# All tap products ahead of the fifth half product, sums of y ahead of the output, and a product's copy split over two buffers

## The chip, the cores and the metric

The kernel runs on one core of a Trainium2 chip. The metric is the device time of one execution in microseconds (us). The kernel before takes 988.49 us, the median of three runs (987.34 to 989.33). The profiled execution, from which all other times here come, has a span of 988.2 us and a mean granted TensorE clock of 0.999.

## The reference

The input x has shape (8, 4224, 192). A causal depthwise convolution with 7 taps, softmax-normalised and one set for each of 8 heads of 24 channels, gives y. Then comes a layer normalisation without bias, a matrix product with w_ch1 (192 x 768), a ReLU, a product with w_ch2 (768 x 192), and y is added again.

```python
# convolution: 7 taps of one head for its 24 channels, softmax over the taps
out = np.einsum('hk,bskhg->bshg', softmax(weight), windows(x_pad))
# mixer
xn = (y - mean(y)) / np.sqrt(var(y) + 1e-06) * g_ln
return y + np.maximum(xn @ w_ch1, 0.0) @ w_ch2
```

All is float32. The kernel folds g_ln and the mean into w_ch1 once, and multiplies by the reciprocal standard deviation only after the second product, since a positive factor passes through the ReLU.

## The kernel before

The rows are cut into 18 groups (numbered 0 to 17); from group 4 on a group is 16 rows on each of 128 partitions. Groups 5 to 16 are called MIXED (line 81), and the change acts on them. The schedule is written by hand: each engine carries out its instructions in the order of the source, and waits only for data and for buffers.

The work on one group g is spread over three rounds of the main loop (line 891). In round g-2 ScalarE makes the first tap product of each head (`first_tap`, line 376, into y) and the second one (`second_tap`, line 393, into the buffer tb), 16 instructions in all, and two DMAs with accumulation then add tb to y (line 403; "y<-tb" in the profile). In round g-1 VectorE adds the other five taps to y (`conv`, line 408), transposes y (`transpose`, line 419) and takes the moments of its rows. In round g TensorE carries out both matrix products.

`up_mixed` (line 591) is the first matrix product of a MIXED group. It is a seven-product scheme on 2 x 2 blocks. The blocks of y are a11 to a22, the precomputed sums of y are s1, s2, s3 (`sums_of_y`, line 575), and the sums of w_ch1 are in w1sums. The steps, numbered 1 to 9 here, are: 1 a11 x b11; 2 a12 x b21; 3 s2; 4 s3; 5 s1; 6 a22; 7 s2 again; then 8 and 9, two plain products for the columns that the scheme leaves out. The steps use two sets of four PSUM banks in turn: 1, 3, 5, 7 and 9 the set `chain`, and 2, 4, 6 and 8 the set `other`. ScalarE copies each result out of its set (`evict`, line 610), and a step can't begin before the copy two steps ahead of it has ended. Steps 2, 5 and 6 are copied to side buffers, from which a DMA with accumulation adds them to a block of the hidden tile `room` (`close`, line 614):

- step 2 to `first`, which lies in the buffer tagged tb, the buffer that the second tap products of another group use too;
- step 5 to `second`, in the buffer tagged cs, which also holds the output columns in `down_fast`;
- step 6 to `first` again.

Each of these two buffers holds three slots of 1024 elements a partition, of which `first` and `second` take two.

`down_fast` (line 714) is the second matrix product, again seven products. Each is a half product of 72 matrix instructions in the profile, numbered 1 to 7 here, and each result but the fourth is copied out by ScalarE in three copies (line 739). Between the half products ScalarE makes tap products of group g+2, as many as `taps_behind` says (line 758). After the fourth, VectorE transposes y of group g+1, and makes the nine `half_sum`s (line 698) that half products 5 to 7 read. After the fifth, `close_by_dma` adds `part` to the block c21 of the output ("cs<-part" in the profile). `finish_fast` (line 796) transposes the output columns from cs to the tile ot, in two halves; the first half needs cs<-part, and the second half (line 801) reads a part that half product 6 left in `room`, which step 3 of the next `up_mixed` writes over. ScalarE scales the rows of ot (line 828) inside the next `up_mixed`, and a DMA with accumulation adds them to the result.

All DMAs with accumulation are issued by GpSimd, in the order of the source.

Of the kernel before, what the change touches and what calls it, by code (L numbers as in the profile page):

```python
# [16 lines left out]
def kernel(  # L17
# [32 lines left out]
    H, K = weight.shape  # L50
# [12 lines left out]
    NQ = P // C  # L63
# [18 lines left out]
    PAIR = NF // 2 - 1  # L82
# [28 lines left out]
    bpool = ctx.enter_context(tc.tile_pool(name="tb", bufs=1))  # L111
    cpool = ctx.enter_context(tc.tile_pool(name="cs", bufs=1))
# [64 lines left out]
    room = hpool.tile([P, NF * J * P], F32, tag="ht", name="room")  # L177
# [213 lines left out]
    tb = {}  # L391
# [16 lines left out]
    def conv(g, k0=1, k1=K, heads=(0, H)):  # L408
        n = groups[g][2]
        t = xg[g]  # L410
        for k in range(k0, k1):
            for h in range(*heads):
                cs = slice(h * GRP, h * GRP + GRP)
                nc.vector.scalar_tensor_tensor(  # L414
                    out=y[g][:, 0:n, cs], in0=t[:, k : k + n, cs], scalar=taps[:, h, k : k + 1],
                    in1=y[g][:, 0:n, cs], op0=ALU.mult, op1=ALU.add,
                )
# [173 lines left out]
    def up_mixed(g, last_sum):  # L591


        W = HJ * C
        assert groups[g][2] == fast[g] == 2 * HJ and PAIR * W == 512
        hidden_tile(g)
        a = ht[g][0]
        a11, a12, a21, a22 = quarters_of_y(g)
        b11, b12, b21, b22 = quarters_of_w1()
        s1, s2, s3 = ysums[g]  # L600
        (c11, c12), (c21, c22) = [
            [a[:, h, e, 0:PAIR].rearrange("p f q j t -> p f q (j t)") for e in range(2)]
            for h in range(2)
        ]

        def parts(pool, tag):
            room = pool.tile([P, J * D], F32, tag=tag, name=f"parts_{tag}{g}")
            return room[:, 0 : PAIR * NQ * W].rearrange("p (f q w) -> p f q w", q=NQ, w=W)

        def evict(banks, dst, relu=False):  # L610
            src = banks.rearrange("p q (f w) -> p f q w", w=W)
            nc.scalar.activation(dst, src, AF.Relu) if relu else nc.scalar.copy(dst, src)  # L612

        def close(c, part):
            whole = "p f q w -> p (f q w)"
            add_by_dma(c.rearrange(whole), part.rearrange(whole))

        def plain(f, banks):
            rows_of_tiles(banks, yt[g][:, 0 : 2 * HJ], w1[:, :, f * P : f * P + P])
            evict_up(g, f, slice(0, 2 * HJ), banks)  # L620


        chain, other = take_set(), take_set()
        turn[0] += 4
        done = groups[g - 1][2]
        first, second = parts(bpool, "tb"), parts(cpool, "cs")
        rows_of_tiles(chain, a11, b11, True, False)
        evict(chain, c11)
        rows_of_tiles(other, a12, b21)
        evict(other, first)  # L630
        close(c11, first)
        rows_of_tiles(chain, s2, w1sums[:, 1], False, False)
        evict(chain, c21)
        scale(g - 1, 0, 1)
        conv(g + 1, 2, 3)
        next(last_sum)
        rows_of_tiles(other, s3, w1sums[:, 2], True, False)
        evict(other, c22)
        scale(g - 1, 1, 2)
        rows_of_tiles(chain, s1, w1sums[:, 0], False, False)  # L640
        evict(chain, second)
        close(c22, second)
        scale(g - 1, 2, 3)
        rows_of_tiles(other, a22, w1sums[:, 3], False)
        evict(other, first)
        close(c21, first)
        scale(g - 1, 3, 4)
        rows_of_tiles(chain, s2, b22, False)
        evict(chain, c12, True)
        nc.scalar.activation(c11, c11, AF.Relu)  # L650
        scale(g - 1, 4, 7)
        conv(g + 1, 3, 6)
        plain(PAIR, other)
        nc.scalar.activation(c22, c22, AF.Relu)
        scale(g - 1, 7, 10)
        add_to_out(g - 1, 0, 8)
        lower_sum(g, (PAIR,))
        lower_sum(g, range(PAIR))
        conv(g + 1, 6, K)
        plain(PAIR + FC, chain)  # L660
        scale(g - 1, 10, done)
        add_to_out(g - 1, 8, done)
# [51 lines left out]
    def down_fast(g):  # L714
        n = fast[g]
        t = width(g)
        w = n * T
        a = ht[g][0]
        flat = cpool.tile([P, NC, NFAST * C], F32, tag="cs", name=f"cs{g}")[:, :, 0 : n * C]
        order = "p c (h j t) -> p c h j t" if t == C else "p c (j h t) -> p c h j t"  # L720
        cs = flat.rearrange(order, h=2, t=t)
        part = cpool.tile([P, CH, NFAST * T], F32, tag="part", name=f"part{g}")[:, :, 0:w]
        part = part.rearrange("p c (j t) -> p c j t", t=t)

        parts = [part, a[:, 1, 0].rearrange("p f q j t -> p (f q) j t")[:, 0:CH]]
        banks = [take_bank() for c in range(CH) for i in range(2)]

        def product(bank, left, right, to, first):
            for c in range(CH):
                dst = banks[2 * c + bank]  # L730
                for f in range(FC):
                    for q in range(NQ):
                        nc.tensor.matmul(  # L733
                            dst[C * q : C * q + C, 0:w], right[:, f, C * c : C * c + C],
                            left[:, f, q], start=(first and f == 0), stop=(f == FC - 1),
                            skip_group_check=True,
                        )
                if to is not None:
                    nc.scalar.copy(  # L739
                        to[:, c], dst[:, 0:w].rearrange("p (j t) -> p j t", t=t)  # L740
                    )

        b = quarters_of_w2()
        c11, c21 = cs[:, 0:CH, 0], cs[:, 0:CH, 1]
        c12, c22 = cs[:, CH:NC, 0], cs[:, CH:NC, 1]
        todo = [(tap, h) for tap in (first_tap, second_tap) for h in range(H)] if g + 2 < NG else []

        def close_by_dma(c, part):
            add_by_dma(*(v.rearrange("p c j t -> p c (j t)") for v in (c, part)))

        def some_taps(times):
            for tap, h in todo[:times]:
                tap(g + 2, heads=(h, h + 1))
            del todo[:times]

        taps_behind = [3, 3, 3, 3, 2, 2]
        if g in MIXED:
            taps_behind = [1, 4, 4, 5, 2, 0]
        elif g + 1 in MIXED:
            taps_behind = [4, 4, 4, 4, 0, 0]  # L760
        product(0, a[:, 0, 0], b[0], c11, True)
        some_taps(taps_behind[0])
        product(1, a[:, 1, 0], w2sums[:, 2], c22, True)
        some_taps(taps_behind[1])
        product(1, a[:, 1, 1], w2sums[:, 3], parts[0], False)
        some_taps(taps_behind[2])
        product(1, a[:, 0, 1], b[2], None, True)
        some_taps(taps_behind[3])
        if g in MIXED:
            transpose(g + 1)  # L770
            moments(g + 1, 0, EARLY)
        elif g + 1 in MIXED:
            moments(g + 1)
            if g + 1 == MIXED[0]:
                sums_of_quarters(w1sums, *quarters_of_w1())
        half_sum(g, (1, 1), (1, 1), (1, 0), ALU.add)
        half_sum(g, (0, 0), (1, 1), (0, 0), ALU.add)
        half_sum(g, (0, 1), (0, 1), (1, 1), ALU.subtract)
        for c in range(CH):
            nc.vector.tensor_tensor(  # L780
                c11[:, c], c11[:, c], banks[2 * c + 1][:, 0:w].rearrange("p (j t) -> p j t", t=t),
                op=ALU.add,
            )
        product(0, a[:, 1, 1], w2sums[:, 1], c21, False)
        if g + 1 == NG:
            finish_fast(g, 0, flat, cs, parts)
        if g in MIXED:
            close_by_dma(c21, parts[0])
        some_taps(taps_behind[4])
        product(0, a[:, 0, 0], w2sums[:, 0], parts[1], False)  # L790
        some_taps(taps_behind[5])
        product(0, a[:, 0, 1], b[3], c12, False)
        some_taps(len(todo))
        return flat, cs, parts
# [96 lines left out]
    for g in range(NG):  # L891
        if g + 2 < NG and g not in (3, 4):
            load_x(g + 2)
        mixed, last = g in MIXED, g + 1 == NG
# [41 lines left out]
        parts = down_fast(g)  # L936
# [6 lines left out]
        if mixed:  # L943
            moments(g + 1, EARLY)
        later = sums_of_y(g + 1) if g + 1 in MIXED else iter(())
        if not last:
            finish_fast(g, 0, *parts)
            next(later, None)
        finish_fast(g, 1, *parts)
        if not last and not mixed and g + 1 not in MIXED:  # L950
            moments(g + 1)
        if not last and g % 2 == 0:
# [35 lines left out]
```

## Time and profile before

| engine | busy us | share of the span | instructions |
|---|---|---|---|
| TensorE, matmul | 969.5 | 98% | 16050 |
| VectorE | 854.3 | 86% | 1477 |
| ScalarE | 623.3 | 63% | 1034 |
| GpSimd | 178.0 | 18% | 317 |

| transfer, issued by GpSimd | issues | KB each | median us from issue to landing |
|---|---|---|---|
| y<-tb | 28 | 768 | 9.1 |
| room<-parts_tb | 24 | 1024 | 9.3 |
| room<-parts_cs | 12 | 1024 | 7.5 |
| cs<-part | 12 | 384 | 4.5 |

In the profile PE is TensorE, PEld its weight loads, ACT ScalarE, DVE VectorE, POOL GpSimd and SP the engine that only issues DMAs. L612 is line 612 of the kernel. A name such as parts_tb<-ps says which tile is written and which is read; ps is PSUM. A row of the waits gives the engine and line that waited, the engine and line (or transfer) that ended the wait, and then the total in us, the number of waits and the longest. A row of the timeline gives the start in us, the us it took, the engine, line and operation, and in brackets the idle time ahead of it with what ended it.

### The profile page before, as it was taken

Reading aid. Unit: us, or ns where it says so; the run is one execution under the profiler, and the core shown is the slowest. Engines: PE = TensorE matmul, PEld = TensorE weight load, DVE = VectorE, ACT = ScalarE, POOL = GpSimd, SP = SyncE. Lnnn points to the kernel's source line nnn. Section 1 sums busy time; section 2 is a strip of 40 time slices with the busy share of each in tenths; the row PEclk is TensorE's granted clock in tenths of the full one; section 3 lists DMA queues with packets and bytes.
Section 4 is the critical chain, followed back from the end, with each engine's and each line's share of the span. In section 5 each row is a group of like instructions: output and inputs, shape, how many; then the busy total and the mean of one; then the engine's idle time right before and its main releaser. Section 6 shows DMA issues by size and latency. Waiting matters only on the chain.

```text
span 988.2 us, 35674 instructions
## 1 busy us (share of the span) xinstructions
PE 969.5 (98%) x16050; PEld 659.8 (67%) x16050; DVE 854.3 (86%) x1477; ACT 623.3 (63%) x1034; POOL 178.0 (18%) x317
## 2 busy tenths in 40 slices
PE   7999999999999999999999999999999999999997
PEld 6886445556758585766758576676857566685787
DVE  6999886899899898989999898989989898998507
ACT  5625646364867758585875858586685848675451
POOL 2002500115111041112211041111301141110200
PEclk9999999999999999999999999999999999999999
DMA  8233752664797869779677977969696786675141
GB/s 201 95 121 130 116 164 36 209 157 130 139 250 145 239 130 191 194 153 253 143 219 145 208 178 143 260 131 241 143 236 148 147 237 135 160 147 93 18 67 67
DMA packets 26279, 156.07 MB, mean 158 GB/s; under 512 B 3215, under 2 KB 8591, under 8 KB 17294
## 3 DMA queue, kind: packets, MB, share of 16 engines
q0 software_dynamic: 19456, 96.25, 50.3%
q1 hardware_dynamic: 6366, 57.54, 15.2%
q8 instruction: 126, 2.06, 0.8%
q14 instruction: 27, 0.22, 0.1%
q10 hardware_dynamic: 304, 0.00, 0.0%
HBM read 38.95 MB, written 50.33 MB: 90 GB/s over the span
## 4 chain that ended last, share of the span: by engine, by line
issue 44%; PE 32%; DMA 11%; POOL 8%; DVE 4%; ACT 2%; POOLq 0%; SPq 0%; ACTq 0%; DVEq 0%
PE ps L532 16%; PE ps L733 11%; DMA y<-tb 7%; PE ps L680 5%; DVE y L414 3%; DMA xg<-in_x_dram 2%; POOL room L589 2%; POOL out_dram L835 2%; POOL cs L589 1%; ACT parts_tb L612 1%; POOL y L403 1%; DMA room<-parts_tb 1%; POOL d L458 1%; DMA ga<-in_moe_g_ln_dram 0%; DVE room L698 0%
## 5 line engine op out<-in xcount | busy, mean ns | idle before, releaser
L414 DVE SCALAR_TENSOR_TENSOR y<-xg,taps,y 128x384 f32<-128x384 f32 (+4 forms) x734 | 368.1, 579 | 12.1 <-issue 8.9
L532 PE MATMUL ps<-yt,w 32*128 32x512 f32 (+5 forms) x4320 | 334.2, 461 | 2.9 <-ACT parts_tb L612 1.9
L532 PEld LDWEIGHTS ps<-yt,w 32*128 32x128 f32 x4320 | 213.7, 185 | 116.5 <-issue 95.4
L733 PE MATMUL ps<-room,w2sums 128*32 128x256 f32 (+2 forms) x4320 | 233.7, 374 | 0.4 <-issue 0.3
L733 PEld LDWEIGHTS ps<-room,w2sums 128*32 128x32 f32 x4320 | 140.9, 110 | 87.7 <-DVE room L698 2.3
L698 DVE TENSOR_TENSOR room<-room 128x1024 f32<-128x1024 f32 (+2 forms) x144 | 160.4, 1186 | 42.0 <-ACT part L739 23.3
L733 PE MATMUL ps<-room,w 128*32 128x256 f32 (+2 forms) x3240 | 179.3, 374 | 0.0
L733 PEld LDWEIGHTS ps<-room,w 128*32 128x32 f32 x3240 | 104.6, 110 | 72.8 <-ACT ot L828 9.1
L739 ACT COPY cs<-ps 128x256 f32<-128x256 f32 (+2 forms) x180 | 63.3, 366 | 111.8 <-PE ps L733 111.1
L522 ACT ACTIVATE room<-ps 128x2048 f32<-128x2048 f32 (+4 forms) x54 | 79.8, 1477 | 55.2 <-PE ps L532 55.1
L532 PE MATMUL ps<-ysums,w1sums 32*128 32x256 f32 x1728 | 98.4, 377 | 4.0 <-ACT parts_tb L612 4.0
L828 ACT ACTIVATE ot<-ot,r 128x192 f32<-128x192 f32 x248 | 96.2, 448 | 0.0
L532 PEld LDWEIGHTS ps<-ysums,w1sums 32*128 32x128 f32 x1728 | 87.5, 185 | 12.8 <-ACT parts_tb L612 8.3
L612 ACT COPY room<-ps 128x2048 f32<-128x2048 f32 x36 | 67.3, 1868 | 39.6 <-PE ps L532 37.1
L707 DVE SCALAR_TENSOR_TENSOR room<-room 128x1024 f32<-128x1024 f32 x36 | 43.0, 1223 | 45.0 <-ACT room L522 24.5
L387 ACT ACTIVATE y<-xg,taps 128x384 f32<-128x384 f32 (+4 forms) x137 | 71.7, 590 | 11.2 <-DMA out_dram<-y 8.5
L835 POOL DMA_DIRECT2D out_dram<-ot x40 | 34.0, 1077 | 238.2 <-ACT ot L828 187.6
L441 DVE BATCH_NORM_STATS2 st<-y 128x6 f32<-128x192 f32 x264 | 70.8, 342 | 0.0
L612 ACT COPY parts_tb<-ps 128x2048 f32<-128x2048 f32 x24 | 44.8, 1866 | 27.3 <-DMA y<-tb 18.5
L803 DVE STREAM_TRANSPOSE ot<-cs 128x512 f32<-128x512 f32 (+2 forms) x90 | 55.8, 670 | 6.2 <-DMA cs<-part 3.7
L425 DVE STREAM_TRANSPOSE yt<-y 128x3072 f32<-128x3072 f32 (+4 forms) x19 | 56.2, 2957 | 5.1 <-PE ps L532 3.0
L400 ACT ACTIVATE tb<-xg,taps 128x384 f32<-128x384 f32 x112 | 59.5, 605 | 0.0
(104 smaller groups left out, 702.4 us busy)
## 6 DMA issues: line engine op xcount, KB each, us to landing
xg<-in_x_dram SPq DMA_DIRECT2D x12, 2112.0 KB, 14.8
room<-parts_tb POOLq DMA_DIRECT2D x24, 1024.0 KB, 9.3
y<-tb POOLq DMA_DIRECT2D x28, 768.0 KB, 9.1
out_dram<-ot POOLq DMA_DIRECT2D x27, 768.0 KB, 7.8
out_dram<-y SPq DMA_DIRECT2D x12, 1536.0 KB, 9.7
room<-parts_cs POOLq DMA_DIRECT2D x12, 1024.0 KB, 7.5
cs<-part POOLq DMA_DIRECT2D x12, 384.0 KB, 4.5
xg<-in_x_dram POOLq DMA_DIRECT2D x2, 2112.0 KB, 17.8
```

Of the source, the lines that this page charges most:

```text
L387: nc.scalar.mul(dst, src, tap)
L400: nc.scalar.mul(tb[g][:, 0:n, cs], xg[g][:, 1 : 1 + n, cs], taps[:, h, 1:2])
L414: nc.vector.scalar_tensor_tensor(out=y[g][:, 0:n, cs], in0=t[:, k : k + n, cs], scalar=taps[:, h, k : k + 1], in1=y[g][:, 0:n, cs], op0=AL ...
L425: nc.vector.transpose(yt[g][:, 0:n, c0:c1].rearrange("p j c t -> p j (c t)"), y[g][:, 0:n, C * c0 : C * c1])
L441: nc.vector.bn_stats(out=sums[g][:, j, :], in_=y[g][:, j, :])
L522: nc.scalar.activation(dst, src, AF.Relu)
L532: nc.tensor.matmul(banks[:, q, i * w : i * w + w], right[rows, c, P * i : P * i + P], left[rows, :, c, :], start=(first and c == 0 and i = ...
L612: nc.scalar.activation(dst, src, AF.Relu) if relu else nc.scalar.copy(dst, src)
L698: nc.vector.tensor_tensor(a[:, *dst, f], a[:, *left, f], a[:, *right, f], op=op)
L733: nc.tensor.matmul(dst[C * q : C * q + C, 0:w], right[:, f, C * c : C * c + C], left[:, f, q], start=(first and f == 0), stop=(f == FC - 1 ...
L739: nc.scalar.copy(to[:, c], dst[:, 0:w].rearrange("p (j t) -> p j t", t=t))
L828: nc.scalar.mul(ots[g][:, j, :], ots[g][:, j, :], rstd[g][:, j : j + 1])
```

## The change

There are four edits, all in the rounds of the MIXED groups.

1. `taps_behind` becomes [1, 4, 4, 7, 0, 0]: the last two of the 16 tap products, which stood behind the copies of half product 5, come ahead of them. With them the issue of y<-tb moves ahead of the issue of cs<-part.
2. In the main loop the sums of y for the next group (the first three subtractions and additions of `sums_of_y`) come ahead of both halves of `finish_fast`, and no longer between them.
3. The copy of step 6 is split in two instructions of 1024 elements a partition. Each goes to the free third slot of one of the two side buffers, and each is closed by a DMA of its own. The copy so no longer writes over the slots that the DMA of step 2 reads.
4. The last tap of `conv` is split by heads: four heads come ahead of step 8 in the source of `up_mixed`, and so ahead of `lower_sum` (line 702) on VectorE, and four stay behind it.

The purpose is to have y<-tb landed when step 2 has to be copied to the same buffer, to spare the copy of step 6 its wait for a DMA, and to have VectorE busy where it waited for ScalarE.

```diff
-            return room[:, 0 : PAIR * NQ * W].rearrange("p (f q w) -> p f q w", q=NQ, w=W)
-        def evict(banks, dst, relu=False):
-            src = banks.rearrange("p q (f w) -> p f q w", w=W)
+            return room.rearrange("p (f q w) -> p f q w", q=NQ, w=W)
+        def evict(banks, dst, relu=False, i=slice(0, PAIR)):
+            src = banks.rearrange("p q (f w) -> p f q w", w=W)[:, i]
...
-        first, second = parts(bpool, "tb"), parts(cpool, "cs")
+        rooms = parts(bpool, "tb"), parts(cpool, "cs")
+        first, second = (r[:, 0:PAIR] for r in rooms)
...
         rows_of_tiles(other, a22, w1sums[:, 3], False)
-        evict(other, first)
-        close(c21, first)
+        for i, room in enumerate(rooms):
+            one, third = slice(i, i + 1), room[:, PAIR : PAIR + 1]
+            evict(other, third, i=one)
+            close(c21[:, one], third)
...
         conv(g + 1, 3, 6)
+        conv(g + 1, 6, K, heads=(0, H // 2))
         plain(PAIR, other)
...
         lower_sum(g, range(PAIR))
-        conv(g + 1, 6, K)
+        conv(g + 1, 6, K, heads=(H // 2, H))
...
         if g in MIXED:
-            taps_behind = [1, 4, 4, 5, 2, 0]
+            taps_behind = [1, 4, 4, 7, 0, 0]
...
-        if not last:
-            finish_fast(g, 0, *parts)
-            next(later, None)
-        finish_fast(g, 1, *parts)
+        next(later, None)
+        for half in range(last, 2):
+            finish_fast(g, half, *parts)
```

## The prediction

> **What bounds the kernel now.** I read the first part of the page, then the waits, then TensorE's timeline group by group, then the other engines in one round. TensorE is busy almost throughout:
>
> ```profile
> PE 969.5 (98%) x16050; PEld 659.8 (67%) x16050; DVE 854.3 (86%) x1477; ACT 623.3 (63%) x1034; POOL 178.0 (18%) x317
> ```
>
> So the time can fall by TensorE's gaps at most. In the view of the waits, these rows matter (total, times, longest):
>
> ```profile
> ACT parts_tb L612 <- DMA y<-tb: 18.5, 11, 2.5
> PE ps L532 <- ACT parts_tb L612: 5.9, 12, 1.2
> ACT parts_tb L612 <- DMA room<-parts_tb: 4.7, 3, 1.6
> DVE ot L803 <- DMA cs<-part: 3.7, 4, 1.7
> ```
>
> ScalarE's copies to the tb buffer wait for two DMAs, and TensorE waits for those copies. The timeline of TensorE in group 14 (steps 1 and 2; 3; 4 and 5; 6; 7; 8 and 9) shows where:
>
> ```profile
> 750.59 5.46 PE L532 MATMUL ps<-yt,w 32*128 32x256 f32 x96
> 755.88 2.77 PE L532 MATMUL ps<-ysums,w1sums 32*128 32x256 f32 x48
> 758.96 5.46 PE L532 MATMUL ps<-ysums,w1sums 32*128 32x256 f32 x96 [0.32 <-ACT parts_tb L612]
> 764.25 2.77 PE L532 MATMUL ps<-yt,w1sums 32*128 32x256 f32 x48
> 766.84 2.77 PE L532 MATMUL ps<-ysums,w 32*128 32x256 f32 x48
> 770.22 10.58 PE L532 MATMUL ps<-yt,w 32*128 32x512 f32 x96 [0.61 <-ACT parts_tb L612]
> ```
>
> An undisturbed step takes 2.59 us from start to start (764.25 to 766.84). Step 4 begins 3.08 us after step 3, so it lost 0.49. Step 8 begins 3.38 after step 7 and lost 0.79. The bracket shows less than is lost, since the modelled ends of matmuls overlap; I count from starts.
>
> The same over all MIXED groups: they begin at 240.31, 296.34, 352.90, 409.43, 466.83, 523.43, 580.59, 637.85, 694.01, 750.59, 808.06 and 865.53, and the last one ends at 922.00, which makes 681.69 us. Group 5, the only one without a wait at step 4, takes 56.03, of which half product 5 loses 0.05: undisturbed is 55.98, times 12 is 671.76. The excess is 9.93. It splits into
>
> - step 4 in groups 6 to 16: 0.48, 0.44, 0.39, 0.43, 1.03, 0.34, 0.19, 0.50, 0.49, 1.39, 0.39, together 6.07, and about 0.10 for each restart where it isn't in the number (9 times, 0.9; steps 4 and 5 then take 5.28 and not 5.18);
> - step 8 in groups 8, 11 and 14: 0.82, 0.83, 0.79, together 2.44, and 0.1 for each restart;
> - half product 5, which waits for VectorE: 0.2.
>
> That is 9.9. Who is late is seen on ScalarE and GpSimd in the round before (the two last second tap products; the two issues; the copy of step 2):
>
> ```profile
> 743.23 1.12 ACT L400 ACTIVATE tb<-xg,taps 128x384 f32<-128x384 f32 x2
> 743.62 1.28 POOL L589 DMA_DIRECT2D cs<-part  x1 [15.14 <-ACT cs L739]
> 744.65 2.08 POOL L403 DMA_DIRECT2D y<-tb  x2
> 757.04 1.87 ACT L612 COPY parts_tb<-ps 128x2048 f32<-128x2048 f32 x1 [1.65 <-DMA y<-tb]
> ```
>
> Step 2 is finished at about 755.9 and ScalarE would be free. The buffer comes free at 757.0.
>
> **What the Trainium skill says.** "DMA: Bandwidth & Descriptors", section "Two DMAs through the same engine are not ordered": descriptors of one queue of one DMA engine start in order. The trace agrees as far as it goes: cs<-part, issued first, lands in 4.5 us though y<-tb follows 1 us later; with the order turned round, cs<-part should queue behind y<-tb. Section "Anatomy of one DMA — SWDGE (gpsimd) path" of the same page puts about 2.0 us of fixed cost on each DMA. Here the transfer engines' busy share rises about 2 us after the issue. "ScalarE: Activation LUTs", section "What ACT_TABLE_LOAD costs", gives 186 ns + 0.833 ns an element, with 93 ns of overlap back to back; the trace has 1.87 us for 2048 elements (1.89 by the page) and 0.37 for 256.
>
> **The change part by part**, in us after the start of a group's round on an undisturbed TensorE. There step 1 begins at 0, step 3 at 5.29, step 4 at 7.88, steps 5, 6, 7 at 10.47, 13.06, 15.65, step 8 at 18.23, half product 1 at 28.64, 2 at 32.55, 4 at 40.32, 5 at 44.21, 6 at 48.1, 7 at 52.0, the end at 55.98. Group 13 lost 0.6 by half product 5, so 694.6 is its zero there.
>
> 1. Taps. After half product 3 ScalarE goes through tap products without a pause until 740.13 (45.5). The two moved ones (1.05 started back to back) end at 46.6; before they ended at 744.35 (49.75). Queued behind them on ScalarE is the first copy of half product 5, which began at 740.37 and now begins 0.8 later. Half product 6 writes that bank at 48.1 and the copy ends at 46.95: no cost. The third copy is made at 48.3 by TensorE's time, as before. GpSimd issues y<-tb at 46.6 instead of 50.05 and cs<-part right behind, at about 49, as before. What moves in all is the same 1920 KB. Before, from the first issue (743.62) to the last landing (757.04) it took 13.4 (13.3 in group 10, 13.4 in groups 5 and 6). Now: y<-tb has landed at the latest at 46.6 + 13.4 = 60.0, 4.0 in the next group; without the 384 KB in front, some 2 earlier. The copy of step 2 needs the buffer at 5.5. Margin 1.5 to 3.5, so the wait at step 4 goes: gain 6.07 + 0.9.
>    The DMA engines are not full then (stretches of two microseconds):
>
> ```profile
> 740.00:742.00 2.00, 2.00 (x44) 1.21 (x40) 2.00 (x3) 0.83 (x3) 0.00 (x0) 1.00 0.98 422
> 742.00:744.00 2.00, 2.00 (x44) 1.17 (x36) 2.00 (x2) 1.08 (x4) 0.38 (x1) 1.00 0.31 126
> 744.00:746.00 2.00, 2.00 (x44) 1.22 (x40) 2.00 (x3) 1.00 (x3) 2.00 (x4) 1.00 0.31 51
> 746.00:748.00 2.00, 2.00 (x44) 1.23 (x40) 2.00 (x7) 0.37 (x1) 0.83 (x2) 1.00 1.23 208
> ```
>
>    The second-last and last column are the DMA share and GB/s: the load of x and the store of y end by 743, and the earlier y<-tb falls into a hole.
> 2. The price is on cs<-part. If it queues behind y<-tb it lands at 60.0, against 48.1 + 0.6 before. VectorE, by its starts in the trace: nine half sums 10.2 from 40.45 (half product 3's end) on, sums into c11 1.0, moments 1.57, sums of y 2.7: it reaches the transposes at 55.9 and waits 4.1. Moving the sums of y ahead puts 2.7 us of work in front of that wait, and gives step 3 its s2 in time. Queued behind the wait: transposes 1.81, line 801 1.05, transposes 1.84, so line 801 ends at 6.9 and ot is ready at 8.7. Step 3's copy, which writes over what line 801 reads, comes at 8.1 (slack 1.2); ScalarE's first scaling of ot at 9.75 (slack 1.0). Then conv and s2 take 17.83, and four heads of the last tap 2.16, to 28.7.
> 3. Step 6. Two copies of 1024 take 0.903 + 1.0 by the slope between the rows for 256 and 2048 elements (1.76 - 0.26 back to back over 1792 elements), from 15.9 to 17.8; one took 1.87. Step 8 needs the set at 18.23: no cost. By the page's price it would be 0.95 + 1.04, also inside. The wait for the DMA of step 2 goes: gain 2.44 + 0.3. Each half needs a DMA issue of 0.86 on GpSimd, which is idle for 9 us behind it. They are issued at about 17.0 and 17.9; a DMA of 1024 KB issued at 18.1 landed by 28.9, so these should land by then. Their rows of 1024 elements instead of 2048 are not priced by the trace; VectorE gets there at 29.9, and half product 1's copies into cs at about 32: margin 1 to 3.
> 4. The last tap. VectorE had gaps of 1.72 and 2.13 (group 13) or, in group 14,
>
> ```profile
> 777.62 1.23 DVE L707 SCALAR_TENSOR_TENSOR room<-room 128x1024 f32<-128x1024 f32 x1 [2.71 <-ACT room L522]
> 780.05 2.36 DVE L707 SCALAR_TENSOR_TENSOR room<-room 128x1024 f32<-128x1024 f32 x2 [1.20 <-DMA room<-parts_tb]
> ```
>
>    Four heads (4 x 0.54 = 2.16) fill them. lower_sum runs 28.7 to 32.2, its first block for half product 2 done at 31.1 (needed at 32.55). Then four heads 2.16, transpose 3.3, moments 2.6: 40.3, just in time for the half sums. So VectorE's work (52.0) and the wait (4.1) fill the 55.98, and it pays for the wait on cs<-part with gaps that it had anyway. The half sums could begin 2.5 later before half product 5 waits.
>
> Sum: 6.97 + 2.74 + 0.2 = 9.9 gained. Small new waits of 0.03 to 0.05 a group I put at 0.4. 988.5 - 9.9 + 0.4 = **979.0**. Groups 0 to 4 and 17 are unchanged but for the order in group 4.
>
> **The rivals.**
>
> A, cs<-part becomes the bound (slower). If the accumulating DMAs are slower in the new order, or overlap with the tail of the load of x, it lands after 5.2 in the next group, line 801 and so step 3's copy come late, and step 5 waits. Landing 2.5 later than I expect (6.5) costs 1.3 for each of 11 groups, 14.3: 988.5 - 9.9 + 14.3 = 993. For it: the slack of 1.2 is small, and in four groups VectorE waits for cs<-part already. Against it: the bytes are the same and the issue comes 3 us earlier, before an idle stretch.
>
> B, only half of it comes. y<-tb is still late in most groups, since the load of x takes the lead, or VectorE's fuller round puts 0.3 to 0.4 a group back: 988.5 - 2.7 = 986 or 988.5 - 9.9 + 4 = 983. Against it: group 5 has no wait at step 4, and the y<-tb ahead of it was made under round 4's list, [4, 4, 4, 4, 0, 0], with all taps ahead of half product 5 (line 760).
>
> C, the copies of step 6 wait after all, for the DMA of step 5 (issued at 16, landing 7.5 later): 6 us for each of 12 groups, 1050. Against it: copies to other parts of `room` go on while a DMA adds to one part (705.33 in group 13, DMA issued at 702.63), so waits go by region.
>
> **How the numbers follow.** Mine 0.74 (977.5 to 982), B 0.13, A 0.10, C 0.01, no change 0.02. The floor is 988.5 - 9.9 = 978.6, less 0.3% of a run's scatter in part: low 977.5. High 986 takes in most of B; outside are A, C and no change. Faster 0.85 (mine and most of B), same 0.04, slower 0.11.
>
> **What would show it.** Right: no wait of parts_tb for y<-tb or for room<-parts_tb; MIXED groups of 56.0 to 56.1; VectorE waiting 3 to 4 us a group for cs<-part; the wait for ScalarE at line 707 gone. Wrong: step 5 of up_mixed waiting behind a copy to room that waits for line 801, or half products waiting for line 698.

## The result, and the profile after

The changed kernel takes 981.24 us (median of four runs, 979.59 to 981.61), the kernel before 988.91 (four runs, 987.34 to 989.85). The ratio is 0.9921 with a 95% interval of 0.9903 to 0.9939, so the gain is between 6.0 and 9.6 us. Forecast were 979.0, with a range of 977.5 to 986.0.

The page after, first the busy times, then the shares of the chain that ended last, by engine:

```profile
PE 967.2 (99%) x16050; PEld 667.1 (68%) x16050; DVE 852.5 (87%) x1477; ACT 624.8 (64%) x1046; POOL 188.3 (19%) x329
PE 94%; DVE 2%; DMA 2%; ACT 1%; issue 0%; SPq 0%; DVEq 0%; ACTq 0%
```

Before, the same row was this:

```profile
issue 44%; PE 32%; DMA 11%; POOL 8%; DVE 4%; ACT 2%; POOLq 0%; SPq 0%; ACTq 0%; DVEq 0%
```

There 44% was time in which the engine on the chain waited for nothing that the profile shows ("issue"), and 11% was transfers. Now it is TensorE from the first groups to the last one. The waits (total, times, longest) show what went and what came:

```profile
ACT parts_tb L613 <- PE ps L532: 13.1, 24, 0.8
DVE ot L808 <- issue: 24.2, 6, 4.5
DVE ot L808 <- DMA cs<-part: 23.1, 6, 4.7
```

ScalarE's copies to the tb buffer wait for no transfer any more, only for TensorE's results. VectorE's first transposes of the output wait 47.3 us, twelve times 3.9, where they waited 3.7 us in all for this transfer. (The trace names the transfer for half of these waits.) The timeline of TensorE in group 14, to be held against the same group before:

```profile
745.67 5.46 PE L532 MATMUL ps<-yt,w 32*128 32x256 f32 x96
750.96 7.95 PE L532 MATMUL ps<-ysums,w1sums 32*128 32x256 f32 x144
758.73 2.77 PE L532 MATMUL ps<-yt,w1sums 32*128 32x256 f32 x48
761.32 2.77 PE L532 MATMUL ps<-ysums,w 32*128 32x256 f32 x48
763.91 10.48 PE L532 MATMUL ps<-yt,w 32*128 32x512 f32 x96
```

Steps 3, 4 and 5 now stand in one row of 7.77 us (750.96 to 758.73), three times 2.59, and step 8 begins 2.59 after step 7. No bracket is left. Why, is seen on the other engines in the same round (GpSimd's two issues; ScalarE's copy of step 2 and the two copies of step 6; VectorE's transposes and lower_sum):

```profile
736.51 1.75 POOL L403 DMA_DIRECT2D y<-tb  x2 [12.93 <-ACT cs L744]
740.45 1.28 POOL L589 DMA_DIRECT2D cs<-part  x1 [2.20 <-ACT room L744]
751.25 1.87 ACT L613 COPY parts_tb<-ps 128x2048 f32<-128x2048 f32 x1 [0.77 <-PE ps L532]
761.56 1.01 ACT L613 COPY parts_tb<-ps 128x1024 f32<-128x1024 f32 x1 [0.33 <-PE ps L532]
762.47 1.02 ACT L613 COPY parts_cs<-ps 128x1024 f32<-128x1024 f32 x1
749.50 1.90 DVE L808 STREAM_TRANSPOSE ot<-cs 128x512 f32<-128x512 f32 x3 [3.81 <-issue]
774.05 3.50 DVE L712 SCALAR_TENSOR_TENSOR room<-room 128x1024 f32<-128x1024 f32 x3
```

y<-tb is issued ahead of cs<-part. The copy of step 2 begins 5.58 after the group's start (745.67), as soon as TensorE is done. The transposes begin 3.83 after it. lower_sum runs without a pause.

A measure that does without the start of the program is the time of the twelve MIXED groups on TensorE, from the first step of group 5 to the first of group 17. Undisturbed it would be 671.76. It was 681.69 before (240.31 to 922.00) and is 672.55 after (241.05 to 913.60): 9.14 gained. The profiled span fell by only 8.4 (988.2 to 979.8), because group 5 began 0.74 later. That start differs between the traces of all kernels here, from 240.3 to 245.3: it is latest (244.5 to 245.3) in the three traces in which the granted clock was 0.50 from about 15 to 22 us, while it is 240.3 to 242.8 in the others, with a clock of 1.00 there. Runs with a mean granted clock of 0.997 or less, as such a start leaves it, took some 2 us longer than the other runs of their kernel.

### The profile page after: what moved, and what is told of

Read it like the earlier page. It is cut to its first block, busy times and chain, and to the rows that moved or that the text cites. A ratio compares the mean times of both kernels' runs of the same rounds, so it can differ in the third digit from the quotient of the medians.

```text
span 979.8 us, 35693 instructions
## 1 busy us (share of the span) xinstructions
PE 967.2 (99%) x16050; PEld 667.1 (68%) x16050; DVE 852.5 (87%) x1477; ACT 624.8 (64%) x1046; POOL 188.3 (19%) x329
## 4 chain that ended last, share of the span: by engine, by line
PE 94%; DVE 2%; DMA 2%; ACT 1%; issue 0%; SPq 0%; DVEq 0%; ACTq 0%
PE ps L532 48%; PE ps L738 41%; PE ps L685 5%; DMA xg<-in_x_dram 2%; DVE y L414 2%; ACT w L355 0%; DMA ga<-in_moe_g_ln_dram 0%; DVE yt L425 0%; DVE y L847 0%; ACT y L387 0%; DVE spare L234 0%; DVE spare L237 0%; ACT spare L221 0%; DVE y L389 0%; DVE ot L872 0%
## 5 line engine op out<-in xcount | busy, mean ns | idle before, releaser
L532 PEld LDWEIGHTS ps<-yt,w 32*128 32x128 f32 x4320 | 217.1, 185 | 110.7 <-issue 90.5
L532 PE MATMUL ps<-ysums,w1sums 32*128 32x256 f32 x1728 | 95.7, 374 | 0.0
L613 ACT COPY room<-ps 128x2048 f32<-128x2048 f32 x36 | 67.2, 1867 | 42.0 <-PE ps L532 41.4
L403 POOL DMA_DIRECT2D y<-tb x28 | 24.6, 1036 | 187.7 <-ACT cs L744 166.7
L685 PE MATMUL ps<-room,w 128*32 128x192 f32 (+3 forms) x1152 | 59.3, 366 | 0.0
```

What stands on the lines that cost most here:

```text
L532: nc.tensor.matmul(banks[:, q, i * w : i * w + w], right[rows, c, P * i : P * i + P], left[rows, :, c, :], start=(first and c == 0 and i = ...
L685: nc.tensor.matmul(bank[C * q : C * q + C, 0:w], w2[:, f, C * c : C * c + C], t[:, f, q, js.start - fast[g] : js.stop - fast[g], :], start ...
```

## The experiments

All edits are numbered as in the section on the change. Ratios are to the kernel before in runs beside it on the same chip (there 991 to 993 us, and 988.91 for the row of the changed kernel); the excess is the time of the MIXED groups over 671.76, from the profile.

| kernel | edits | time us | ratio, 95% interval | excess us |
|---|---|---|---|---|
| before | none | | 1 | 9.93 |
| after | 1 2 3 4 | 981.24 | 0.9921, 0.9903 to 0.9939 | 0.79 |
| e1_taps | 1 | 1021.07 | 1.0288, 1.0258 to 1.0319 | 37.65 |
| e2_taps_sums | 1 2 | 983.99 | 0.9920, 0.9903 to 0.9937 | 0.80 |
| e3_split | 3 | 988.18 | 0.9962, 0.9947 to 0.9976 | 6.11 |
| e4_no_tap_split | 1 2 3 | 981.68 | 0.9896, 0.9879 to 0.9913 | -0.06 |
| e5_order | 1 2 3 4, issues turned round | 988.91 | 0.9977, 0.9965 to 0.9989 | 5.38 |
| e7_no_taps | 2 3 4 | 989.15 | 0.9966, 0.9956 to 0.9977 | 5.99 |
| e6_junk384 | 1 2 3 4, cs<-part delayed | 986.14 | 0.9919, 0.9889 to 0.9949 | 2.05 |
| e8_junk1152 | 1 2 3 4, delayed more | 1004.01 | 1.0108, 1.0077 to 1.0139 | 21.90 |
| e9_junk_no_split | 1 2 3, delayed more | 996.93 | 1.0064, 1.0044 to 1.0083 | 14.47 |
| r1_all_four | 1 2 3 4 | 983.00 | 0.9918, 0.9904 to 0.9932 | 0.35 |
| r2_taps_sums | 1 2 | 983.54 | 0.9927, 0.9913 to 0.9940 | 1.52 |
| r3_no_tap_split | 1 2 3 | 984.09 | 0.9920, 0.9907 to 0.9934 | -0.06 |

### Does cs<-part queue behind y<-tb? Edit 1 alone

```diff
-            taps_behind = [1, 4, 4, 5, 2, 0]
+            taps_behind = [1, 4, 4, 7, 0, 0]
```

> Edit 1 alone (all 16 tap products ahead of half product 5), the other three edits undone. My theory, that cs<-part queues behind y<-tb: y<-tb lands in time, so the waits at step 4 (7.0 us in all) go. But cs<-part lands about 4.0 us into the next group, and the sums of y now stand behind the transposes that wait for it, so s2 is ready at about 7.8 and step 3, due at 5.29, begins some 2.6 late in each of 11 groups: 988.9 - 7.0 + 28 = about 1010, slower than before; since steps 6 to 8 slip too, the 2.7 of step 8 may go as well (1007). Rival, that the two transfers share the engines and cs<-part still lands 4.5 us after its issue: no wait at step 3, 982 to 984.

It is slower by 2.9%. TensorE waits, 25.7 us in eleven groups by the waits, for the second of the sums of y. The timelines of TensorE (first two rows) and VectorE, the first in group 6 and the second ahead of group 7 (which begins at 358.90):

```profile
298.72 5.46 PE L532 MATMUL ps<-yt,w 32*128 32x256 f32 x96
306.42 9.74 PE L532 MATMUL ps<-ysums,w1sums 32*128 32x256 f32 x144 [2.24 <-DVE ysums L582]
...
362.80 1.90 DVE L803 STREAM_TRANSPOSE ot<-cs 128x512 f32<-128x512 f32 x3 [6.49 <-DMA cs<-part]
364.62 0.92 DVE L581 TENSOR_TENSOR ysums<-yt 128x768 f32<-128x768 f32 x1
365.57 0.96 DVE L582 TENSOR_TENSOR ysums<-ysums,yt 128x768 f32<-128x768 f32 x1
```

The transposes wait for cs<-part until 3.90 after the start of the group, and the sums of y stand behind them. Step 3 begins 7.70 after step 1 instead of 5.29, 2.4 late. The mechanism is as expected, and the rival, by which cs<-part would land in 4.5 us again, has fallen: it takes 10.7. The loss is larger than expected, 37.7 us and not 28. The starts give 27.7 for the eleven late steps 3 (2.1 to 2.9 each). Most of the rest is in the second row above: 9.53 us for steps 3 to 5 (306.42 to 315.95), where 7.77 is the rule. In five of the eleven groups they took 9.53 or 9.54, 8.8 us in all. Some 1.2 us are spread over other steps. Stretches of the group in that row; the third number from the end is the granted clock:

```profile
304.40:306.40 2.00, 0.00 (x0) 0.01 (x1) 1.97 (x4) 1.76 (x1) 0.00 (x0) 1.00 0.00 0
306.40:307.40 1.00, 0.98 (x10) 1.00 (x14) 1.00 (x2) 0.00 (x0) 0.90 (x1) 0.55 0.00 0
307.40:308.40 1.00, 1.00 (x16) 1.00 (x12) 0.90 (x2) 0.00 (x0) 0.00 (x0) 0.50 0.63 131
308.40:309.40 1.00, 1.00 (x15) 1.00 (x12) 1.00 (x3) 0.00 (x0) 0.00 (x0) 0.50 1.29 262
309.40:310.40 1.00, 1.00 (x20) 1.00 (x19) 1.00 (x3) 0.00 (x0) 0.00 (x0) 0.74 0.75 156
310.40:311.40 1.00, 1.00 (x24) 1.00 (x20) 1.00 (x3) 0.36 (x1) 0.00 (x0) 1.00 1.14 238
```

TensorE paused for some 2.2 us, and then had half its clock for about 3.4.

### Is it the order of issue, or the place of the tap products?

All four edits, but with the DMAs of the second tap issued by a function of their own behind the close of c21; ScalarE's order is that of the change:

```diff
-        if heads[1] == H:
+        if heads[1] == H and g - 2 not in MIXED:
+            add_second(g)
...
             close_by_dma(c21, parts[0])
+            if g + 2 < NG:
+                add_second(g + 2)
```

> All four edits, but the issue of y<-tb is put behind the issue of cs<-part on GpSimd; the tap products on ScalarE stay where the change put them. My theory, that the order of issue decides which transfer lands first: cs<-part lands some 4.5 us after its issue again and VectorE's wait of 4 us a group is gone or short, but y<-tb is issued at about 50 and lands at about 62.4, 6.4 us into the next group, where the copy of step 2 needs the buffer at 5.5: the losses at step 4 are back at 0.4 to 0.6 a group. 0.8% (7 us) less gain than with all edits, ratio to before 0.997 to 0.998. Rival, that the two moved tap products on ScalarE are what counts: as with all edits, ratio 0.990 to 0.992.

The median time from issue to landing of cs<-part (last number) is first that of the changed kernel and then that of this one:

```profile
cs<-part POOLq DMA_DIRECT2D x12, 384.0 KB, 10.7
```

```profile
cs<-part POOLq DMA_DIRECT2D x12, 384.0 KB, 4.5
```

The same transfer of the same bytes lands 6.2 us earlier when it is issued ahead. The price is on the other one; the waits of this kernel:

```profile
ACT parts_tb L617 <- DMA y<-tb: 15.9, 10, 2.1
PE ps L536 <- ACT parts_tb L617: 2.6, 8, 0.8
```

The copy of step 2 waits for y<-tb again, and the excess is 5.38. The ratio of 0.9977 lies in the expected range. So the moved tap products bring nothing by themselves; they matter because the issue of y<-tb has to wait for them. For cs<-part it is the place in the queue that decides, since it is issued at about the same time in both kernels (49.0 to 50.8 us after the group's start). For y<-tb this run doesn't part the place in the queue from the time of issue: it lands 5.4 to 6.9 us into the next group instead of 0.8 to 2.4, and most of that is that it is issued 3 to 5 us later.

The opposite test leaves out edit 1 and keeps the other three:

```diff
-            taps_behind = [1, 4, 4, 7, 0, 0]
+            taps_behind = [1, 4, 4, 5, 2, 0]
```

> Edits 2, 3 and 4 without edit 1 (two tap products stay behind half product 5). My theory: the losses at step 4 stay as before (6 to 7 us), those at step 8 are gone, and edits 2 and 4 move nothing: 3.8 us less than before as with edit 3 alone, ratio 0.995 to 0.998. Rival, that edit 2 or 4 frees something by itself: ratio under 0.994.

Measured 0.9966, and an excess of 5.99, with ten waits of the copies for y<-tb (16.5 us). Edits 2 and 4 free nothing that shows without edit 1: this is the result of edit 3 alone, within the interval.

### What each of the other edits is worth

Edits 1 and 2, with the output half of the diff as it stands in the section on the change:

```diff
-        if not last:
-            finish_fast(g, 0, *parts)
-            next(later, None)
-        finish_fast(g, 1, *parts)
+        next(later, None)
+        for half in range(last, 2):
+            finish_fast(g, half, *parts)
```

> Edits 1 and 2 (taps, and sums of y ahead of the output); the copy of step 6 is whole and the last tap too. My theory: the waits at step 4 go (-7.0), the waits of step 8 for the DMA of step 2 stay in some groups (2.7 in all before): 988.9 - 7.0 = 981.9, and up to 984 if more groups than three wait there, now that nothing delays step 6. VectorE waits about 4 us a group for cs<-part. Rival, that VectorE becomes the bound without the split last tap: half product 5 waits for line 698, 0.3 to 1 us a group, 985 to 993.

The ratio is that of the full change, 0.9920. Edit 2 turns a loss of 2.9% into a gain of 0.8%, by nothing but the order of three sums and three transposes on VectorE. Of the losses at step 8 one group kept its own, group 11, on ScalarE and TensorE:

```profile
598.05 1.86 ACT L612 COPY parts_tb<-ps 128x2048 f32<-128x2048 f32 x1 [1.34 <-DMA room<-parts_tb]
...
599.97 10.58 PE L532 MATMUL ps<-yt,w 32*128 32x512 f32 x96 [0.40 <-ACT parts_tb L612]
```

Step 8 begins 3.17 after step 7 (596.80), 0.58 late. Before, three groups had it, with 0.8 each. Edit 1 gives this wait a little more room: before, step 6's copy in group 14 was due 7.9 us after the issue of the DMA of step 2 (759.21 to 767.1), here in group 11 it is 8.2 (588.89 to 597.08). The landing took 9.0 and 9.1. In most other groups the same transfer takes 7.0 to 7.8 and lands in time; which groups get the long one is not explained (before 8, 11 and 14, here 11).

Edit 3 alone:

> Edit 3 alone: the copy of step 6 in two instructions to the third slots. My theory: the losses at step 8 in groups 8, 11 and 14 go (2.44 + 0.3), the losses at step 4 stay (6 to 7): 986.2. Rival, that the two copies or the two smaller DMAs cost something: step 8 or line 707 late, 988 to 990. Rival, that step 8's loss only moves to step 4: 988.9.

The ratio of 0.9962 is a gain of 2.4 to 5.3 us, and the excess fell by 3.82, to 6.11. ScalarE's waits for room<-parts_tb are gone, those for y<-tb remain:

```profile
ACT parts_tb L612 <- DMA y<-tb: 17.5, 11, 2.1
PE ps L532 <- ACT parts_tb L612: 3.1, 8, 0.8
```

More was gained than the 2.74 expected for step 8, since y<-tb also came a little less late in this execution: it cost TensorE 6.1 and not 7.0 at step 4, and nothing in group 12. The split itself costs nothing that can be seen.

Edits 1, 2 and 3, without the split of the last tap:

> Edits 1, 2 and 3 without the split of the last tap. My theory: VectorE gets its gap back ahead of lower_sum and is about 1 to 1.5 us later at the half sums (41.4 and not 40.45 after the group's start), and half product 5 needs the first at 44.2: no cost for TensorE, 981.2 as with all four edits, at most 0.3 more. Rival, that VectorE is the bound with the wait on cs<-part: half product 5 loses 0.3 to 1 us a group, 984 to 993.

Measured 0.9896, and no excess. VectorE ahead of and at the half sums of the group that begins at 690.21:

```profile
716.32 2.35 DVE L710 SCALAR_TENSOR_TENSOR room<-room 128x1024 f32<-128x1024 f32 x2
719.22 1.23 DVE L710 SCALAR_TENSOR_TENSOR room<-room 128x1024 f32<-128x1024 f32 x1 [0.54 <-DMA room<-parts_cs]
...
730.65 10.29 DVE L701 TENSOR_TENSOR room<-room 128x1024 f32<-128x1024 f32 x9
```

lower_sum begins at 26.1 after the group's start here and at 28.4 (group 14) with the split. The half sums begin at 40.44 here (41.4 was expected) and at 39.97 there, and half product 5, which reads them from 44.2 on, loses nothing in either. So edit 4 earns nothing: it fills VectorE's gap (0.54 in the rows above), but nobody waits for the half sums that come 0.5 earlier by it, and lower_sum comes 2.3 later.

The three were run once more, beside each other on one chip:

> The changed kernel with all four edits once more, beside the two that follow on the same chip. If edits 1 and 2 carry nearly all, as the traces so far say (rounds of the MIXED groups 672.6 us with all four and with edits 1 and 2 alone, 671.7 without edit 4, 681.7 before): ratio to before 0.989 to 0.992, and the three kernels within 1 us of each other. If edits 3 and 4 earn what was forecast for them (2.7 and 0.2 us): this one 2 to 3 us ahead of edits 1 and 2 alone.

> Edits 1 and 2 alone, again. Traces so far: one group in twelve loses 0.7 us at step 8, so 0.7 to 1.0 us behind all four edits. By the forecast for edit 3: 2.7 us behind.

> Edits 1, 2 and 3, again. Theory that VectorE has slack: equal to all four edits within 0.5 us. Theory that the split of the last tap earns something: 1 us or more behind.

The medians are 983.00, 983.54 and 984.09, and the intervals of the ratios overlap almost wholly: the times can't tell them apart. By the excess, edits 1 and 2 alone stand 1.2 us behind all four in these traces, with two groups that take 0.7 longer than the others; the kernel without edit 4 has none, as in its first run, and owes its slower time here to its start (group 5 begins at 244.67).

### How much slack is left? cs<-part delayed by one more transfer

A transfer from a constant tile to a scratch tensor that nothing reads is put between y<-tb and cs<-part:

```diff
+    spill = nc.dram_tensor("spill", (len(MIXED), P, 768), F32).ap()
+
+    def junk(g, w):
+        nc.gpsimd.dma_start(
+            out=spill[g - MIXED[0]][:, 0:w], in_=w1.rearrange("p c f -> p (c f)")[:, 0:w]
+        )
...
+            junk(g, 768)
             close_by_dma(c21, parts[0])
```

> All four edits, and one more transfer of 384 KB from a constant tile to a scratch tensor in HBM, issued by GpSimd between y<-tb and cs<-part in every MIXED round (the output does not use it). It delays cs<-part: by 1.0 us if it goes at the 420 GB/s that plain transfers reach, by 1.9 at the 205 of the accumulating ones, and GpSimd issues it a microsecond later in any case. Line 806 now ends 6.6 to 7.0 after the group's start, and step 3's copy may begin at 8.1: the slack is 1.1 to 1.5. My theory (the slack is real and small): 0 to 0.5 us a group lost at step 5, 0 to 6 us in all, ratio 0.991 to 0.998. Rival, that cs<-part has no slack: 1 to 2 us a group, ratio 1.003 to 1.015.

Its excess is 2.05. The transposes begin 4.7 to 5.3 us after the group's start, 5.0 on the mean of eleven groups (2.9 to 4.3 and 3.8 in the changed kernel), and nothing is lost at step 5. The loss is at another place, half product 2 behind lower_sum, as in group 14 (which begins at 749.95):

```profile
782.50 0.61 PE L745 MATMUL ps<-room,w2sums 128*32 128x256 f32 x8
783.37 7.54 PE L745 MATMUL ps<-room,w2sums 128*32 128x256 f32 x136 [0.25 <-DVE room L712]
```

Half products 2 and 3 take 8.24 there (782.50 to 790.74) and not 7.77.

With 1152 KB, the same with `junk(g, 2304)` and a scratch tensor of that width:

> As the run with 384 KB more, with 1152 KB: cs<-part is late by 2.9 (plain rate) to 5.8 us (accumulating rate). My theory: beyond a slack of 1.1 to 1.5 us each microsecond of lateness is paid at step 5 of up_mixed, and so the loss is 1.4 to 4.5 us for each of 12 groups: 981 + 17 to 54 = 998 to 1035, ratio 1.007 to 1.045, with TensorE waiting at step 5 for ScalarE's copy, which waits for line 806. Rival, that VectorE's half sums give out instead: the waits of TensorE are at half products 5 to 7, behind line 703.

The excess is 21.9, 2.0 for each of eleven groups. The waits of TensorE:

```profile
PE ps L532 <- ACT room L613: 10.5, 11, 1.2
PE ps L745 <- DVE room L712: 5.5, 11, 0.5
```

and, in the group that begins at 703.56, what the first one stands behind:

```profile
710.52 1.90 DVE L816 STREAM_TRANSPOSE ot<-cs 128x512 f32<-128x512 f32 x3 [6.28 <-DMA cs<-part]
712.34 0.92 DVE L814 TENSOR_TENSOR cs<-cs,room 128x768 f32<-128x768 f32 x1
...
713.34 1.87 ACT L613 COPY room<-ps 128x2048 f32<-128x2048 f32 x1 [2.34 <-DVE cs L814]
```

The transposes begin 6.96 after the group's start, line 814 (line 806 of the changed kernel) ends at 9.7, step 3's copy begins at 9.8 instead of 8.1, and step 5 is 1.23 late (715.26 less 708.85 and two steps), as the prediction's rival A had it. But half product 2 loses another 0.7 (8.48 instead of 7.77, from 737.49 to 745.97), behind lower_sum, which none of the theories named.

That second loss is edit 4's, if lower_sum is late because of the four heads in front of it. So once more with the last tap whole behind lower_sum:

```diff
-        conv(g + 1, 6, K, heads=(0, H // 2))
...
-        conv(g + 1, 6, K, heads=(H // 2, H))
+        conv(g + 1, 6, K)
```

> The run with 1152 KB more ahead of cs<-part, with the last tap whole behind lower_sum again (edit 4 undone). With the split it lost 21.9 us in the MIXED rounds, about 1.3 a group at step 5 (behind line 814) and 0.6 at half product 2 (behind lower_sum, line 712). My theory, that edit 4 earns nothing and only puts 2.2 us of work in front of lower_sum: the loss at half product 2 goes, that at step 5 stays: MIXED rounds 686 to 688 us, about 6 to 7 us faster than with the split, ratio 1.002 to 1.006. Rival, that the split gives VectorE time that it needs when it is late: the loss moves to half product 5 and is as large or larger, 693 us and more, ratio 1.010 and more.

```profile
PE ps L532 <- ACT room L613: 8.8, 11, 1.1
```

The wait behind lower_sum is gone; the MIXED groups take 686.23, 7.4 us less than with the split. A little of it moved to half product 5: in the group that begins at 699.91, half products 5 and 6 take 7.98 (745.26 to 753.24), 0.21 more than undisturbed. So with cs<-part 3.1 us later edit 4 costs 7.4 us. The loss of e6_junk384 stands behind lower_sum as well, but that kernel was not run without the split.

## Why the prediction was right

**The bound.** TensorE's gaps were the whole of the possible gain, and counting them from starts gave 9.93; 9.14 of it came in the profile.

**Edit 1.** y<-tb was expected to have landed by 4.0 at the latest, with the copy of step 2 at 5.5. It is there in time in every group, 0.8 to 2.4 us after the group's start, and the copy begins at 5.58, when TensorE is done. e5_order and e7_no_taps show that this is the part which carries the gain, since without the earlier issue 5.4 to 6.0 us of the excess stay; e1_taps shows that it does so only together with edit 2.

**Edit 2 and the price on cs<-part.** Expected: landing at 60.0, a wait of 4.1, line 801's end at 6.9. Measured: the transposes begin 3.8 into the next group on the mean of eleven (2.9 to 4.3), the wait is 3.9, and the line (806 in the changed kernel) ends 6.6 (group 14) and 7.0 (group 13) after the group's start. The Trainium skill's page "DMA: Bandwidth & Descriptors", section "Two DMAs through the same engine are not ordered", from which the queueing was taken, says that the descriptors of one queue start in order, and the trace agrees: cs<-part landed 4.5 us after its issue ahead of y<-tb and 10.7 behind it. Rival A names a real limit: e8_junk1152 shows it at step 5 when the transposes begin 3.1 us later. The slack of 1.2 at step 3's copy was about right, too. What I missed is that lower_sum at half product 2 gives out first: e6_junk384, 1.2 later, loses there already and not at step 5. I had put its margin at 1.4, for the first block; the second block ends later, and that is the one that TensorE waits for in the trace.

**Edit 3.** The copies take 1.01 us each and begin 0.91 apart, as worked out. The term that was mis-sized is its gain of 2.74 in the sum. With edits 1 and 2 alone only 0.80 and 1.52 us of excess are left, one and two slow groups instead of three, so beside them edit 3 is worth about 1 us in the profile; alone it brought 3.8, of which the 2.7 at step 8 are its own. The 0.3 us more of room that edit 1 gives takes about 0.2 from each loss (0.58 to 0.66 instead of 0.8). The larger part is that fewer of the transfers took 9 us, one and two of twelve instead of three; whether edit 1 does that or chance is open. The sum doesn't suffer, since with both edits the loss at step 8 is gone whichever of them is credited with it.

**Edit 4.** Said to fill gaps, with "just in time" behind it and no gain of its own but a share of 0.2 at half product 5. The half sums do begin in time, at 39.8 to 40.4 where 40.3 was forecast. But without the split TensorE loses nothing either, so the edit is worth nothing (e4_no_tap_split, r3_no_tap_split), and it costs margin (e8_junk1152 against e9_junk_no_split).

**The sum.** 9.5 forecast, 7.7 between the medians, 8.4 between the profiled spans, 9.14 in the MIXED groups. The allowance of 0.4 was 0.79: it all stands between 453 and 494 us, from half product 5 of group 8 to step 9 of group 9, where the matmuls take a little longer without a wait that the profile names. The same kernel had 0.35 of it in r1_all_four, between 466 and 494 us. What it is stays open; it is not the small new wait in every group for which the 0.4 was allowed. The 0.74 ahead of group 5 belongs to the start, and the rest of the difference to 7.7 lies within the scatter of the runs, which is about 2 us from lowest to highest.

Rival B, half of the gain, didn't come: no MIXED group has a wait at step 4 or 8. Rival C, copies that wait by whole buffer, has fallen: the copies of step 6 begin 0.33 and 0 us after what is ahead of them, though the DMA of step 5 out of the same cs buffer is in flight (group 13: issued at 705.21, copy into that buffer at 706.50, median landing 7.2 after the issue).

## What to carry to other kernels

When two transfers go through one queue, find out whose consumer comes first, issue that one first, and then move work that others need ahead of the wait for the other one; the first half of this without the second cost 2.9% here, both together gained 0.8%. When two losses are mended at once, measure each with the other one mended: what was counted as 2.7 us before was about 1 us then. And an edit that fills a gap with work which is due later puts that work in front of what is due sooner; ask what stands behind the gap.

## What the runs showed of the hardware that was not expected

A pause of TensorE can cost more than its length. In e1_taps the pauses ahead of step 3, 1.9 to 2.7 us by the trace, were followed in five groups of eleven by 3.41 us at a granted clock of 0.50, which cost 1.76 us each. Whether it happened did not go by the length: it came where step 3 was 2.4 late and not where it was 2.9 late. It went by where the pause fell. The five slow stretches begin at 306.51, 367.95, 487.41, 664.91 and 842.40 us, and the distances between them are 18, 35, 52 and 52 times 3.413. When the whole span is laid out in windows of that length, TensorE was idle for 2.07 to 2.57 us of the window just ahead of each slow stretch; in the other six groups the pause fell across two windows, with at most 1.93 us in one (the ends of matmuls are modelled, so these are not exact). The pauses of up to 1.4 us in the kernel before and in e8_junk1152 left the clock at 1.00. The Trainium skill ("TensorE: Matmul & The Clock Gate", section "Part 1: The HAM clock gate (the "warmup" mystery)") gives a half clock after an idle window of about 3.4 us that runs free of the program. The length of the slow stretch and the windows agree; but here a window didn't have to be idle as a whole, about 2 us of it were enough.

Accumulating transfers moved 197 to 236 GB/s with the transfer engines fully busy (746 to 754 us in the kernel before), the plain loads and stores ahead of them 405 to 445 (734 to 742 us; stretches of 2 us each), so that an accumulating transfer was about twice as dear in queue time as a plain one of its size. The plain 384 KB of e6_junk384 delayed the transposes by 1.2 us, the 1152 KB of e8_junk1152 by 3.1 in the group shown.
